# The opening of a fused attention and MLP kernel: modulation products before the transposes, loads in pieces over both queues, dummies behind gates

## The chip, the cores and the metric

The kernel runs on one core of a Trainium2 chip (trn2). The metric is the device time of one execution in microseconds (us).

Three instruction streams matter in what follows. PE is the matrix engine (TensorE), DVE the vector engine, POOL the GpSimd engine; ACT (the scalar engine) and SP (the sync engine) also issue transfers, each on a queue of its own.

## The reference, cut to what matters

```python
mod = (_silu(c) @ w_mod).reshape(c.shape[0], 6, 1, -1)
sa, ca, ga, sb, cb, gb = ...                     # six vectors of 512
h = _layernorm(x, axis=-1) * (1 + ca) + sa       # x: 2048 x 512
x = x + ga * attention(h, k_cache, v_cache, wq, wo)   # 32 heads, the last 512 keys
h = _layernorm(x, axis=-1) * (1 + cb) + sb
x = x + gb * (relu(h @ w1) @ w2)
```

Before any head can be projected (q = h @ wq), the first 512 rows of x must be normalised, transposed, and scaled by `1 + ca` and shifted by `sa`. These two vectors come from `silu(c)` and the first 1,024 columns of `w_mod` (1 MB).

## The kernel before

Each engine has an instruction stream, and a small builder (`KB`) works out the semaphore waits. It walks through the program in the order of the Python calls, and keeps for each resource its last write and the reads since. An operation waits for what has been recorded up to then.

```python
for r in reads:
    req(r.w)               # the last write recorded so far; None: no wait
for w in writes:
    req(w.w)
    for ev in w.r:         # the reads recorded so far
        req(ev)
```

The opening (cut; "..." marks cuts):

```python
for i in range(2):                                   # x, tiles 0..3, in two transfers
    dma(x_sb[:, 2*i:2*i+2, :], xv[:, 2*i:2*i+2, :], f"xa{i}", writes=..., eng=ACT if i else SP)
dma(c_row[:, :], ...)                                # c, 1 KB, on SP
load_wm01(0); load_wm01(1, ACT)                      # w_mod, two halves of 512 KB
load_wq(0, 2, ACT); load_wq(2, 2); load_k(0); load_v(0)
kb.op(POOL, ... memset(ones, 1.0))
...
warm(7)                  # 7 dummy products of 512 columns on PE
silu_exp(5)              # transpose of c on PE, exp on ACT; waits for c
warm(9)                  # 9 more dummies
...
silu_mul()               # POOL: three operations, result sc_bf
ln_stat(0); ln_stat(1)   # DVE: mean and variance of tiles 0 and 1, result mv
rstd_add(0, 2); rstd_pow(0, 2)                       # DVE, then a power on POOL
ln_stat(2) ...
ln_norm(0); ln_norm(1)                               # DVE: xn
...
ln_tposes(0, TB[0])      # PE: 4 transposes of tile 0
fs = mod_cols_mm(0, QBK) # PE: 32 one-column products, w_mod x silu(c)
for f in fs: f()
ln_norm(2)
mod_cols_evac(0, QBK)    # DVE: modc, the scale and shift
for tl in range(1, TPB): ln_tposes(tl, ...)
# then: hT = xnT * scale + shift in two halves, and the projections of heads 0 and 1
```

The dummies are there for PE's clock, which starts low: at first they stand 0.43 us apart, later 0.22.

## Time and profile before

| | before |
|---|---|
| median of the first 3 runs | 560.43 us (560.34 to 561.92) |
| median of 6 runs, taken beside the changed kernel | 560.94 us (560.34 to 562.04) |
| span of the profiled run | 559.4 us |
| PE busy | 98% of the span |
| first score product (attention proper begins) | 13.34 us |

How to read it: PE is busy nearly all the time. The lines themselves stand in the prediction below. In them `psW<-ones` is a dummy, `psQ<-sc_bf,wmw` a modulation product (`wmw` is w_mod), `<-ident,xn` a transpose, `<-hT,wq` a projection and `psS<-qT,kT` a score product; psW, psQ, psO and psS are the banks that PE writes, and modc is the scale and shift. Nearly all products pass through one helper (L1372) and nearly all transposes through another (L1375). A mean clock of 1.000 is the full one.

### The profile page before, as it was taken

To read this page: it belongs to the slowest core of one execution; us is meant where nothing else is said; L and a number is where in the kernel's file an instruction comes from. 1 tells how busy PE (TensorE), PEld (TensorE's weight loads), DVE (VectorE), ACT (ScalarE), POOL (GpSimd) and SP (SyncE) were. 2 spreads that over 40 slices of the span, in tenths; PEclk is the share of its full clock that TensorE was granted. 3 is DMA by queue.
4 is the path that set the end of the run, shared out by engine and by line. 5 is a ranking of instruction groups with operands and counts; after the bars stand their busy time and mean duration, and the time that the engine had idled before them with its cause. 6 is when DMAs were issued, how large, how long until landed. Compare 5 with 4: busy or idle time off the path is not lost.

```text
span 559.4 us, 9666 instructions
## 1 busy us (share of the span) xinstructions
PE 550.5 (98%) x4060; PEld 315.8 (56%) x4134; DVE 253.8 (45%) x551; ACT 348.9 (62%) x453; POOL 54.7 (10%) x53
## 2 busy tenths in 40 slices
PE   8999999999999999999999999999999999999998
PEld 4665555555555555555555555555555654444444
DVE  4455555553546544335445443333354448321134
ACT  4986666666666666666666666666666644432500
POOL 3000022004410000033000000332000000000000
DMA  9897763513114144352352412111215110210001
GB/s 268 248 207 174 143 169 46 114 39 76 40 38 76 39 73 117 58 133 57 94 95 57 76 40 39 39 39 38 39 39 76 39 30 0 44 34 23 22 29 47
DMA packets 113309, 42.67 MB, mean 76 GB/s; under 512 B 93928, under 2 KB 112104, under 8 KB 113256
## 3 DMA queue, kind: packets, MB, share of 16 engines
q1 hardware_dynamic: 112024, 40.82, 34.3%
q10 hardware_dynamic: 1232, 1.15, 0.6%
q8 instruction: 33, 0.54, 0.4%
q14 instruction: 20, 0.16, 0.1%
HBM read 18.35 MB, written 2.10 MB: 37 GB/s over the span
## 4 chain that ended last, share of the span: by engine, by line
PE 98%; issue 1%; DMA 1%; DVE 0%; SPq 0%; DVEq 0%
PE psS L1372 28%; PE psO L1372 27%; PE psQ L1372 23%; PE psW L1372 20%; DMA c_row<-in_c_dram 1%; DVE qT L1611 0%; DVE hT L1630 0%; SPq L1303 0%; DVE PT L1723 0%; DVE PT L1725 0%; PE psS L1375 0%; PE psO L1416 0%; DVE modc L1438 0%; DVEq L123 0%
## 5 line engine op out<-in xcount | busy, mean ns | idle before, releaser
L1493 ACT ACTIVATE PT<-psS 128x1024 bf16<-128x1024 f32 x256 | 262.7, 1028 | 128.2 <-PE psS L1372 128.1
L1372 PE MATMUL psS<-qT,kT 128*128 128x512 bf16 x508 | 150.9, 379 | 0.5 <-DVE qT L1611 0.4
L1372 PEld LDWEIGHTS psO<-v,PT 128*128 128x128 bf16 x2048 | 126.6, 98 | 30.2
L1372 PE MATMUL psO<-v,PT 128*128 128x129 bf16 x2048 | 137.0, 220 | 0.0
L1372 PE MATMUL psQ<-hT,wq 128*128 128x512 bf16 (+1 forms) x510 | 130.5, 377 | 0.3 <-DVE hT L1630 0.2
L1503 DVE RECIPROCAL rinv<-psO 128x4 f32<-128x4 f32 x128 | 23.3, 182 | 227.2 <-PE psO L1372 227.2
L1372 PE MATMUL psW<-wo,oT 128*128 128x512 bf16 x454 | 118.1, 379 | 3.0
L1504 DVE TENSOR_TENSOR o<-psO,rinv 128x512 bf16<-128x512 f32 x128 | 88.5, 691 | 4.9 <-DVE rinv L1503 0.5
L1372 PEld LDWEIGHTS psQ<-hT,wq 128*128 128x128 bf16 x512 | 49.9, 98 | 60.3 <-issue 0.6
L1372 PEld LDWEIGHTS psS<-qT,kT 128*128 128x128 bf16 x512 | 49.5, 98 | 58.9 <-ACT PT L1493 0.7
L1485 ACT ACTIVATE qT<-psQ 128x512 bf16<-128x512 f32 x126 | 74.7, 593 | 0.0
L1712 ACT ACTIVATE wq<-psS 128x512 bf16<-128x512 f32 x56 | 33.4, 597 | 49.3 <-PE psS L1372 48.9
L1372 PEld LDWEIGHTS psW<-wo,oT 128*128 128x128 bf16 x512 | 45.0, 98 | 32.9 <-DVE acc L1526 1.2
L1526 DVE TENSOR_TENSOR acc<-psW,acc 128x512 f32<-128x512 f32 x48 | 33.2, 691 | 6.5 <-PE psW L1372 6.5
L1372 PE MATMUL psO<-wmw,wq 128*128 128x512 bf16 (+1 forms) x165 | 32.8, 352 | 0.3
L1529 POOL TENSOR_TENSOR acc<-acc,gaf 128x512 f32<-128x512 f32 x12 | 15.6, 1303 | 146.7 <-DVE acc L1526 139.8
L1388 POOL TENSOR_TENSOR rstd<-rstd,cst 128x4 f32<-128x4 f32 x7 | 7.2, 1025 | 216.8 <-DVE rstd L1387 216.8
L1723 DVE TENSOR_TENSOR PT<-psO,gbf 128x512 f32<-128x512 f32 (+1 forms) x12 | 7.5, 624 | 40.4 <-PE psO L1372 40.4
L1372 PE MATMUL psS<-h2T,wmw 128*128 128x512 bf16 x109 | 25.0, 379 | 0.2
L1372 PEld LDWEIGHTS psO<-wmw,wq 128*128 128x128 bf16 x168 | 15.3, 98 | 16.5
L1372 PE MATMUL psS<-hT,wmw 128*128 128x512 bf16 x110 | 24.4, 379 | 0.1
L1382 DVE BATCH_NORM_STATS2 st<-x 128x6 f32<-128x512 bf16 x31 | 21.1, 681 | 4.8 <-DMA x<-in_A_x_dram 4.8
(85 smaller groups left out, 192.6 us busy)
## 6 DMA issues: line engine op xcount, KB each, us to landing
wo<-in_A_wo_dram SPq DMA_DIRECT2D x4, 1024.0 KB, 5.9
wq<-in_A_wq_dram SPq DMA_DIRECT2D x7, 512.0 KB, 4.6
wmw<-in_B_w_dram SPq DMA_DIRECT2D x14, 256.0 KB, 3.1
wmw<-in_w_mod_dram SPq DMA_DIRECT2D x5, 512.0 KB, 4.8
oT<-o SPq DMA_TRANSPOSE x128, 2.4
out_dram<-PT SPq DMA_DIRECT2D x15, 128.0 KB, 1.7
x<-in_A_x_dram SPq DMA_DIRECT2D x3, 512.0 KB, 4.3
v<-in_A_v_cache_dram SPq DMA_DIRECT2D x8, 128.0 KB, 3.8
```

Of the source, the lines that this page charges most:

```text
L1372: kb.op(PE, lambda e: e.matmul(out_ap, lhsT, rhs, start=start, stop=stop), reads=reads, group_writes=[R_b[k] for k in bk], signal=signal)
L1382: kb.op(DVE, lambda e: e.bn_stats(st[:, t, :], x_sb[:, t, :]), reads=[R_x[t]], writes=[R_st[t]])
L1388: kb.op(POOL, lambda e: e.tensor_tensor(rstd[:, sl], rstd[:, sl], cst[:, 0:1].to_broadcast([P, hi - lo]), op=ALU.pow), reads=R_rstd[sl] + ...
L1485: kb.op(ACT, lambda e: e.activation(qT[u % NQT][:, :], bank[bk], ACTF.Copy), reads=[R_b[bk]], writes=[R_qT[u % NQT]])
L1493: kb.op(ACT, lambda e: e.activation(PT[u % NPT][:, pr * 2:pr * 2 + 2, :], s_ps[pr][:, :, :], ACTF.Exp, scale=scale), reads=[R_b[pr * 2], R ...
L1503: kb.op(DVE, lambda e: e.reciprocal(rinv[:, u, :], o_ps[:, :, P]), reads=[R_b[5], R_b[6]], writes=[R_rinv])
L1504: kb.op(DVE, lambda e: e.tensor_tensor(o_sb[u % NOS][:, :, :], o_ps[:, :, 0:P], rinv[:, u, :].unsqueeze(2).to_broadcast([P, TPB, P]), op=A ...
L1526: kb.op(DVE, lambda e: e.tensor_tensor(acc[:, tl, :], bank[WBK], acc[:, tl, :], op=ALU.add), reads=[R_b[WBK], R_acc[tl]], writes=[R_acc[tl]])
L1529: kb.op(eng, lambda e: e.tensor_tensor(acc[:, tl, :], acc[:, tl, :], gaf[:, :], op=ALU.mult), reads=[R_acc[tl], R_ga], writes=[R_acc[tl]])
L1712: kb.op(ACT, lambda e: e.activation(h1T[b % 2][:, fc, :], bank[bk], ACTF.Relu), reads=[R_b[bk]], writes=[R_h1[b % 2][fc]], pre=all_events( ...
L1723: kb.op(DVE, lambda e: e.tensor_tensor(yt[i][:, c0:c1], bank[bk][:, c0:c1], gbf[:, c0:c1], op=ALU.mult), reads=[R_b[bk], R_gb], writes=[R_ ...
```

## The change

Its intent: let the modulation products run while PE would otherwise wait for the first normalised tile; bring x and w_mod in smaller pieces so that work can begin on the first ones; keep PE occupied with dummies only as long as needed (gated by the statistics of tiles 0 and 1). The diff, cut to its core:

```diff
     def load_wm01(i, eng=None):
-        c0, c1 = i * DC // 2, (i + 1) * DC // 2
-        dma(wm01[:, c0:c1, :], wm01v[:, c0:c1, :], f"wm{i}", writes=[R_wm[i]], eng=eng)
+        dma(wm01[:, i, :], wm01v[:, i, :], f"wmc{i}", writes=[R_wmc[i]], eng=eng)
...
-    def warm(n):
+    def warm(n, gate=()):
         for i in range(n):
-            mm(bank[WBK], ones..., [R_ones], [WBK], i == n - 1)
+            mm(bank[WBK], ones..., [R_ones] + list(gate), [WBK], i == n - 1)
...
     for i in range(2):
-        dma(x_sb[:, 2 * i:2 * i + 2, :], ..., f"xa{i}", ..., eng=ACT if i else SP)
+        for t in (2 * i, 2 * i + 1):
+            dma(x_sb[:, t, :], xv[:, t, :], f"xa{t}", writes=[R_x[t]], eng=ACT if i else SP)
     dma(c_row[:, :], ...)
-    load_wm01(0)
-    load_wm01(1, ACT)
-    load_wq(0, 2, ACT)
+    for i in range(DC):
+        load_wm01(i, (ACT, SP)[i % 2])
+    for i, eng in enumerate((ACT, SP)):
+        dma(wq_sb[:, 2 * i:2 * i + 2, 0:QA * Dh], ..., f"wqa{i}", writes=[R_wqa[i]], eng=eng)
...
-    kb.op(POOL, lambda e: e.memset(ones[:, :], 1.0), writes=[R_ones])
+    kb.op(DVE, lambda e: e.memset(ones[:, :], 1.0), writes=[R_ones])
...
-    warm(7)
+    warm(10)
     silu_exp(5)
-    warm(9)
+    warm(3, [R_mv[0]])
+    warm(2, [R_mv[1]])
...
-    ln_tposes(0, TB[0])
     fs = mod_cols_mm(0, QBK)
     for f in fs:
         f()
+    ln_tposes(0, TB[0])
+    mod_cols_evac(0, QBK)
     ln_norm(2)
-    mod_cols_evac(0, QBK)
```

## The prediction

> **What bounds the kernel now.** I read the page first, for what limits the whole span, then the chain of waits for the first 14 us, the timeline of the same stretch, and last the landing times of the opening loads. The page's part 1 and part 4:
>
> ```profile
> PE 550.5 (98%) x4060; PEld 315.8 (56%) x4134; DVE 253.8 (45%) x551; ACT 348.9 (62%) x453; POOL 54.7 (10%) x53
> ...
> PE 98%; issue 1%; DMA 1%; DVE 0%; SPq 0%; DVEq 0%
> ```
>
> PE is busy 98% of 559.4 us and the chain lies on it. In the steady part one step of attention costs PE about 2.63 us (projections in the chain start at 20.82, 23.45, 26.14, 28.72), with no gap over 0.05 us. The diff touches no instruction of that part except the resources its waits name, so what it can win is the time before PE starts streaming. The chain of waits there (start us, us, what):
>
> ```profile
> 1.24 3.66 DMA c_row<-in_c_dram
> 4.90 0.05 issue
> 4.95 0.18 PE psO L1416
> 5.13 3.86 PE psW L1372 x9
> 8.98 0.22 PE psS L1375 x4
> 9.21 0.79 PE psQ L1372 x32
> 10.00 0.02 issue
> 10.02 0.18 DVE modc L1438
> ...
> 10.30 0.42 DVE hT L1630
> ...
> 12.55 0.44 DVE qT L1611
> 12.99 0.35 issue
> 13.34 0.38 PE psS L1372
> ```
>
> So the opening is 13.3 us, 2.4% of the time, and it would have to shrink by 11.2 us for a 2% gain. What stands on it: the nine dummy products (psW), which begin when c has landed and keep PE until 8.8; four transposes; the 32 modulation products; their evacuation (modc); the scaling of hT; the first projections. Is PE needed there, or only occupied? The timeline, in which the bracket tells what ended a wait:
>
> ```profile
> 6.92 0.20 POOL L1423 TENSOR_TENSOR sc_bf<-c_f,tmp 128x4 bf16<-128x4 f32 x1
> 7.08 1.51 POOL L1591 TENSOR_TENSOR rstd<-rstd,cst 128x2 f32<-128x2 f32 x2
> 7.82 1.22 DVE L1393 TENSOR_SCALAR xn<-x,mv,rstd 128x512 bf16<-128x512 bf16 x3
> 8.02 0.15 PEld L1372 LDWEIGHTS psW<-ones 128*128 128x128 bf16 x1 [0.28 <-issue]
> 8.70 0.90 POOL L1604 TENSOR_SCALAR xn<-x,s,rstd 128x512 bf16<-128x512 bf16 x1
> 9.04 0.94 PE L1372 MATMUL psQ<-sc_bf,wmw 128*128 128x1 bf16 x32
> 10.02 0.17 DVE L1438 TENSOR_TENSOR modc<-psQ,m 128x8 f32<-128x8 f32 x1 [0.98 <-PE psQ L1372]
> ```
>
> sc_bf is ready at 7.12 and the first xn at about 8.24, yet neither gets a PE slot before 8.82: dummies hold it. The loads the products need:
>
> ```profile
> wmw<-in_w_mod_dram SPq DMA_DIRECT2D x1, 512.0 KB, 6.3
> ```
>
> That half, issued at 1.66, lands at 1.66 + 6.3 = 7.96; the half on ACT's queue was issued at 1.23 and took 4.9, so 6.13. First x lands at 0.79 + 4.0 = 4.79 and 0.79 + 4.2 = 4.99.
>
> **What the Trainium skill says.** "TensorE: Matmul & The Clock Gate", Part 1, says that the array starts at half clock and gets the full one only after a busy window of about 3.4 us, in a window that runs freely. The trace agrees in effect: dummy weight loads stand at 5.46, 5.89, 6.32 ... 8.02, 0.43 us apart for 512 columns, while later 512-column products are 0.215 us apart; the granted clock nevertheless reads 1.00, so that column doesn't show it. The switch comes only near 8.5, since the first seven dummies stop at 4.2 and the wait for c breaks the window. "DMA: Bandwidth & Descriptors", "Issuing engines are not separate DMA queues", says that SP's and ACT's transfers share 16 engines, and a second queue saves issue time alone. It agrees: the windows view has these engines at 1.01 to 1.16 of busy share from 3 to 8 us, at 326 to 385 GB/s. Spreading loads only reorders bytes. The same page, "Queues, rings and completion order", has each engine consume a queue's descriptors in ring order; c (1 KB), issued right after x on SP, lands at 4.90, after x's 4.79, as that says.
>
> **The change part by part.**
> *Ones on DVE.* POOL's memset ran 0.78 to 0.98 and PE began at 1.04. DVE is free from the start; I take 0.1 us for it: PE begins near 0.93.
> *Ten dummies before the silu transpose, not seven.* Ten at 0.425 are 4.25 us: PE is free at 5.2. Before, c alone set that transpose, at 4.94. So +0.25 on the silu chain, a loss. It should also fill a clock window, so the switch comes near 5.2, or by 7.6 at worst.
> *x in four transfers, c behind two of them.* c's issue moves from 1.24 to about 1.65, yet it still follows the same 256 KB in its ring. x rows become 1 KB pieces, so I allow 0.1 to 0.4: c at 5.0 to 5.3. With PE free at 5.2, the silu transpose is at about 5.25: +0.3 on before. Tile 0 alone lands about 1 us earlier, near 3.8, and statistics finish earlier; but that buys nothing, as POOL's power for rstd stands behind the three silu operations in program order (5.43 to 7.12), and those start with c. POOL's chain so moves +0.3: sc_bf 7.42, first rstd 8.1, xn0 8.55, xn1 8.87, xn2 9.35, xn3 (before 8.70 to 9.60) 9.9.
> *Loads of w_mod in four chunks, alternating.* x and w_mod are 1.5 MB. From 1 to 7 us the windows view moved 27+215+361+385+378+366 = 1,732 KB, 1.5 MB by about 6.5; add the spread between engines and the 1 KB rows: the last chunk lands at 7.2 to 7.5 rather than 7.96, no longer mixed with wq.
> *Gated dummies.* Three wait for tile 0's statistics (ready), two for tile 1's (about 6.0). At the half clock they end at 7.5, at the full one at 6.5. Neither holds xn0 back.
> *Products ahead of the transposes.* They run 7.5 to 8.35, beside POOL and DVE instead of on the path; their evacuation comes after xn1 in DVE's order, 8.77 to 8.95.
> Then: transposes of tile 1 done about 9.35, so the first half of hT starts near 9.4, against 10.28: -0.9. The transposes of tile 3 wait for POOL's xn3 at 9.9 and are done at 10.35, so the second half starts at 10.4 (before 10.95). Three DVE scalings 0.32 apart end at 11.45; the last four second-half products of 0.109 end their stream at 12.0, the qT cast runs 12.2 to 12.6 (before 12.99 to 13.41): 0.8 us earlier.
>
> Sum: products and evacuation off the path -1.0, dummies that held the first transpose (8.82 against 8.24 + 0.2) -0.4, later c and silu +0.3, tile 3 through POOL as the new limit +0.3: -0.8 us. From there PE streams as before, all of it reaching the end: 560.43 - 0.8 = 559.6.
>
> **The rivals.** (1) The silu chain eats it: if c lands at 5.8, behind 256 small pieces, everything behind POOL moves by 0.9 and the gain is about 0.2: 560.2. For it: c's landing is on the chain already, and its ring isn't shortened. Against: it comes behind the same bytes. (2) The last w_mod chunk stays at 8.0: the products end at 8.85 and now stand ahead of the transposes, so tile 0 waits 0.3; but the second half hangs on xn3 at 9.9, so only 0.1 is lost: 559.7. (3) Cold clock: fewer dummies (15 for 16), maybe a pause before 7.5. If the first projections ran at 0.213 instead of 0.109 each, 16 would cost 1.7 us more: 561.3. Against: over 6 us of nearly unbroken dummies hold a full window at most phases. (4) POOL is not the limit as I have it, or the switch comes so early that all is ready sooner: the gain is 1.2 and the time 559.2. (5) Later loads hide the gain: the third projection needs wq for heads 2 and 3 (landed about 9.2) and kT (about 9.8), both ahead of 12.2; SP issues kT some 1.3 us later, behind three more issues, so it stays inside. I give that little.
>
> **Range and chances.** -0.8 with half a microsecond of doubt from c, the phase of the clock window (which can also shorten the dummies of before in some runs) and the spread of three runs (560.34 to 561.92). Nothing is 11 us large. 558.9 to 560.5 should hold it; within 2% almost surely.
>
> **What would show it.** In the changed profile: ten dummies from about 0.93; c or the tenth dummy as what released the silu transpose at about 5.25; sc_bf at 7.4; 32 products before 8.5, beside POOL; the first scaling of hT near 9.4; the last transposes waiting on POOL's xn; the first score product near 12.5; the same 2.63 us step behind it; span about 558.6. I am wrong if c lands past 5.6, if the products wait past 8.0 for w_mod, if projections come 0.21 apart, or if the opening gets shorter and the span doesn't.

## The result, and the profile after

The changed kernel takes 563.11 us at the median (562.78 to 563.69, 6 runs) against 560.94 us of the kernel before (6 runs); the ratio is 1.0037, with a 95% interval of 1.0023 to 1.005. It is about 2.1 us slower where 0.8 us faster was forecast. The change stays inside 2%, but the sign is wrong and the time lies above the range.

The profiled run spans 561.0 us. The chain of waits of the changed kernel (start us, us, what), to be held against the chain of before in the prediction:

```profile
2.20 7.41 DMA wmw<-in_w_mod_dram
9.61 0.05 issue
9.65 0.57 PE psQ L1373 x16
10.22 0.02 issue
10.24 0.17 DVE modc L1439
10.41 0.33 DVE xn L1394
...
11.64 0.85 PE psQ L1373 x4
12.49 1.71 PE psO L1373 x8
14.20 0.61 PE psQ L1373 x4
14.81 0.21 issue
15.02 0.38 PE psS L1373
```

Two things are to be seen. The chain now hangs on a transfer of w_mod, which is issued at 2.20 and lands at 9.61; before, the later half of w_mod was issued at 1.66 and was there at 7.96. (In front of the lines shown, from 0.80 to 2.20, ACT issues two pieces of x and the first chunk, one after another: more pieces also mean a later issue.) And the eight half-width projections into psO take 1.71 us; in the chain of the run that changed only the order, which is shown further down, the same eight take 0.89. The first score product comes at 15.02 instead of 13.34: 1.68 us later, and the span is 561.0 - 559.4 = 1.6 us longer. So all of it is in the opening. From the first score product to the end both kernels take 546 us (559.4 - 13.34 = 546.1; 561.0 - 15.02 = 546.0).

Why do the projections take twice as long? The windows view of the changed kernel gives, for each stretch, the length, then the busy time (and number of instructions) of PE, weight loads, DVE, ACT and POOL, then the granted clock of PE, the busy share of the DMA engines, and GB/s:

```profile
6.00:7.00 1.00, 0.25 (x2) 0.00 (x0) 0.93 (x4) 0.97 (x3) 0.92 (x2) 1.00 0.84 311
7.00:8.00 1.00, 0.00 (x0) 0.00 (x0) 0.93 (x4) 0.31 (x2) 0.76 (x2) 1.00 1.08 352
...
11.00:12.00 1.00, 1.00 (x11) 0.88 (x9) 0.76 (x3) 1.00 (x3) 0.00 (x0) 0.51 1.23 243
12.00:13.00 1.00, 1.00 (x7) 0.69 (x6) 0.73 (x3) 0.63 (x2) 0.00 (x0) 0.50 1.09 335
13.00:14.00 1.00, 1.00 (x7) 0.69 (x6) 0.00 (x0) 0.38 (x1) 0.00 (x0) 0.50 1.22 294
```

PE does nothing from 6.25 to beyond 8, and from about 11.0 its clock is granted at 0.50, until about 14.4. The records of the clock in this trace put the half-clock stretch at 11.03 to 14.44: 3.41 us. In that stretch start all but the last of the 16 half-width projections of the first two heads (11.43 to 14.54).

The timelines of PE part the 1.68 us. The first projection starts at 11.43 instead of 10.86, 0.57 us later; from there to the first score product it is 3.59 us instead of 2.48, 1.11 us more. So in this one run the late start costs about a third and the half clock about two thirds.

The third view is the timeline of the changed kernel:

```profile
1.11 3.84 PE L1373 MATMUL psW<-ones 128*128 128x512 bf16 x10 [1.11 <-DVE ones L1571]
...
4.88 0.17 PE L1417 MATMUL psO<-ident,c_row 4*128 4x4 bf16 x1
...
4.99 1.26 PE L1373 MATMUL psW<-ones 128*128 128x512 bf16 x5
...
5.92 0.18 DVE L1384 BATCH_NORM_AGGREGATE mv<-st 128x2 f32<-128x6 f32 x1 [1.71 <-PE psW L1373]
...
6.85 0.20 POOL L1424 TENSOR_TENSOR sc_bf<-c_f,tmp 128x4 bf16<-128x4 f32 x1
...
8.41 0.75 PE L1373 MATMUL psQ<-sc_bf,wmw 128*128 128x1 bf16 x16 [2.16 <-DMA wmw<-in_w_mod_dram]
...
9.65 0.55 PE L1373 MATMUL psQ<-sc_bf,wmw 128*128 128x1 bf16 x16 [0.49 <-DMA wmw<-in_w_mod_dram]
```

The five "gated" dummies run straight behind the silu transpose and take 1.26 us together: they wait for nothing. The line at 5.92 shows the opposite of a gate: the statistics of tile 0 (whose first step ended at 4.21) stood still for 1.71 us until dummies (psW) had run. That is the builder's rule from above. `warm(3, [R_mv[0]])` is called before `ln_stat(0)`, so no write of mv is recorded yet and the read waits for nothing; the later write of mv then has to wait for the reads. The gate points backwards.

So there were three suspects: the late w_mod, the fall of the clock, and the backward gates.

### The profile page after: what moved, and what is told of

Same layout as the page of the kernel before. It is cut to its first block, busy times and chain, and to the rows that moved or that the text cites. A ratio compares the mean times of both kernels' runs of the same rounds, so it can differ in the third digit from the quotient of the medians. Undisturbed runs are those within 1.5% of the kernel's fastest.

```text
span 561.0 us, 9673 instructions
## 1 busy us (share of the span) xinstructions
PE 550.4 (98%) x4059; PEld 316.5 (56%) x4133; DVE 253.9 (45%) x552; ACT 349.1 (62%) x453; POOL 54.5 (10%) x52
## 4 chain that ended last, share of the span: by engine, by line
PE 97%; DMA 1%; issue 1%; ACTq 0%; DVE 0%
PE psS L1373 28%; PE psO L1373 27%; PE psQ L1373 23%; PE psW L1373 19%; DMA wmw<-in_w_mod_dram 1%; ACTq L1303 0%; PE psS L1376 0%; DVE xn L1394 0%; DVE PT L1727 0%; DVE PT L1729 0%; PE psW L1376 0%; DVE modc L1439 0%
```

## The experiments

Each changes the kernel before or the changed kernel by a few lines; all results were correct. The theory (T in the expectations) was that the loss comes from the late w_mod and from the clock together. The rivals: late loads alone (L), the clock alone (C), the backward gates (G), the order (O).

### First round

**e_fill.** The changed kernel, more dummies.

```diff
     warm(2, [R_mv[1]])
+    warm(14)
```

> The changed kernel with 14 more dummy products behind the gated ones, nothing else. Theory T (the 2 us come from two things: the clock of TensorE falls to half from 11.0 to 14.4 us because PE stands idle from 6.2 to 8.4, and the last chunk of w_mod lands at 9.6): granted clock 1.00 throughout, projections 0.109 us apart again, span about 559.4, ratio to before 0.999 to 1.001; the modulation products still wait for w_mod until about 9.6. Rival L (late loads alone cost it, the clock is incidental): nothing gained, ratio stays near 1.0037. Rival C (the clock alone costs it): ratio 0.999 or lower, with products not late.

Measured: 562.57 us, ratio 1.003 (1.0017 to 1.0043), clock 1.00 in all five runs. In the profiled run, the fastest of the five (span 559.8), the clock went as T has it: the projections were 0.109 us apart and the first score product came at 13.51. But w_mod landed at about 9.1, and what the products waited for were the dummies, which ended at 9.18. The mean is far worse than that run. Fourteen dummies take 14 x 0.22 = 3.1 us at full clock and 14 x 0.43 = 6.0 us at half, and in the traces the clock rises anywhere from 3.8 to 13.3 us; a fixed number of dummies may so pay back what it buys. That this is what made the other four runs slow is not shown, since only one was traced. By its ratio, T missed.

**e_oldloads.** The changed kernel with the opening loads of before.

```diff
-    x in four transfers, w_mod in four, wq for heads 0 and 1 in two
+    x in two transfers, w_mod in two halves, wq for heads 0 and 1 in one (as before)
```

> The changed kernel with the opening loads of before (x in two transfers, w_mod in two halves, wq for two heads in one), dummies and order as changed. Theory T: w_mod lands near 8.0, the products run 8.0 to 8.8, the projections start about 1.3 us earlier than in the changed kernel; PE still idles from 6.2 to 8.0, so the clock may still fall, at a moment when fewer projections are left: ratio 1.000 to 1.002. Rival L: back to before or better, 0.998 to 1.000, even if the clock falls. Rival C: clock below 1.00 and ratio still 1.003.

Measured: 562.07 us, ratio 1.0017 (1.0005 to 1.0029). w_mod landed at 8.00 and the products ran from 8.14 to 9.1, about as expected. Of six runs five had a mean clock of 0.997 and took 561.91 to 562.95 us; the sixth had 1.000 and took 560.98. One kernel, one chip, and the runs whose clock fell lie 562.31 - 560.98 = 1.3 us above the one whose clock did not. (This is not the fall alone: the moment at which the clock first rises also differs from run to run and sets how long the dummies last.) The profiled run also showed the backward gates at work: its clock rose only at 6.9, so the dummies were slow, and the statistics behind them waited until 7.17. From there the chain runs through the statistics to the transposes, not through w_mod.

**e_fill_oldloads.** Both undone.

```diff
     (loads as in e_oldloads)
     warm(2, [R_mv[1]])
+    warm(9)
```

> The changed kernel with the loads of before and 9 more dummies (to about 8.0 us): both suspected causes undone, the products still ahead of the transposes. Theory T: the gain that was predicted appears, clock 1.00, span about 558.6, ratio 0.998 to 0.999. If a third cause exists, the ratio stays at 1.000 or above.

Measured: 561.28 us, ratio 1.0009 (0.9996 to 1.0022), clock 1.00 in all runs. T missed here too. The profiled run had a span of 558.8, close to the 558.6 that the prediction promised, but it was the fastest of five; the spans went up to 560.1. In it the gain that was predicted is there; what takes it away in the other runs was not traced. Even in this run the chain passes through a backward gate: the aggregate of tile 0 starts at 5.85, released by dummies that end at 5.75.

**e_newloads_only.** The kernel before with only the changed loads.

```diff
-    x in two transfers, w_mod in two halves, wq for heads 0 and 1 in one
+    x in four transfers, w_mod in four, wq for heads 0 and 1 in two (as changed)
```

> The kernel before with only the changed opening loads (x in four transfers, w_mod in four chunks, wq for two heads in two, over both queues). Its dummies run until about 8.8 and the transposes stand ahead of the products. Theory T: products finish at about 10.05 instead of 9.85 since the last chunk lands near 9.6, clock stays 1.00, ratio 1.0003 to 1.001. Rival L: the whole loss, 1.003 to 1.004. Rival C: 1.000 or below.

Measured: 561.15 us, ratio 1.0004 (0.9991 to 1.0016). The last chunk landed at about 9.8 and the products ended near 10.3, about as expected. Late w_mod by itself is nearly free under the old order. In the profiled run it does set the pace (the first score product comes at 13.61, 0.27 us later than in the trace of before), but four transposes go ahead of it and the clock stays up, although the dummies ended at 7.1. Rival L, as a cause by itself, falls.

### Second round

**e_order_only.** The kernel before with only the changed order.

```diff
-    ln_tposes(0, TB[0])
     fs = mod_cols_mm(0, QBK)
     for f in fs:
         f()
+    ln_tposes(0, TB[0])
+    mod_cols_evac(0, QBK)
     ln_norm(2)
-    mod_cols_evac(0, QBK)
```

> The kernel before with one edit: the 32 modulation products and their evacuation ahead of the transposes of tile 0. Theory T (the order is harmless, the loss comes from the loads and the clock): products start when the dummies end (about 8.8 at the half clock) and end by 9.6, the first half of hT is scaled some 0.1 to 0.2 us earlier, ratio 0.9993 to 1.000. Rival O (the order itself costs it, since the transposes now wait behind w_mod): ratio 1.001 or more.

Measured: 560.54 us, ratio 0.9994 (0.998 to 1.0007), clock 1.00. The order is harmless and perhaps worth 0.3 us, which is within the noise. Lines of its chain of waits:

```profile
1.65 6.18 DMA wmw<-in_w_mod_dram
...
7.97 0.95 PE psQ L1372 x32
...
10.77 0.89 PE psO L1372 x8
...
12.26 0.59 PE psS L1372 x2
```

The products now wait for w_mod (7.83) and nothing else, and the scores begin at 12.26. That run's clock had risen by about 3.9 us, so that its nine dummies were over at about 7. In the trace of before that the prediction was read from, the clock rose only near 8.8 and the dummies held PE until then. The spread of the kernel before may well come from this; only one run of it was traced, so that is not shown.

**e_realgate.** The changed kernel with the gates recorded after what they name.

```diff
-    warm(3, [R_mv[0]])
-    warm(2, [R_mv[1]])
...
     ln_stat(0)
     ln_stat(1)
+    warm(3, [R_mv[0]])
+    warm(2, [R_mv[1]])
```

> The changed kernel with the two gated groups of dummies recorded after the statistics they name, so that the wait goes the meant way. As changed, the builder sees these reads of mv before anything writes it: the dummies wait for nothing, and the writing of mv waits for the dummies (in the changed profile the aggregate of tile 0 starts at 5.92, 1.7 us after its statistics, released by PE psW). Theory T: that inversion was hidden behind w_mod at 9.6 and the clock, so the aggregate moves to about 4.4, xn0 to about 7.8, and the time stays: ratio 1.002 to 1.004. Rival G (the inverted wait is the cause): ratio 1.000 to 1.001.

Measured: 562.88 us, ratio 1.0038 (1.0024 to 1.0052). The aggregate of tile 0 moved from 5.92 to 4.61, right behind its statistics, and nothing was won: the first xn began at 8.36 (8.02 in the changed kernel), and the last chunk landed at about 9.7. In the profiled run the clock fell for two windows (9.13 to 15.96). The backward gates are a real error in the code, but rival G falls as the cause of this loss. Where w_mod is on time they do show: the chains of e_oldloads, e_fill_oldloads, e_after_xpairs and e_dummies_only pass through them; what they cost there was not measured by itself.

**e_wmchunks.** The kernel before with w_mod in four chunks, nothing else.

```diff
-    load_wm01(0)
-    load_wm01(1, ACT)
+    for i in range(DC):
+        load_wm01(i, (ACT, SP)[i % 2])
```

> The kernel before with w_mod in four chunks over both queues and nothing else of the loads changed; one look at when the last chunk lands. If the chunks themselves are what comes late: 9.0 or later. If it is the four transfers of x ahead of them: 8.2 or earlier. The time of one run decides nothing.

Measured: one run of 560.79 us (state unknown). The last chunk on SP's queue, from the issues view (tile, queue, size, us from issue to landing), issued at 2.05:

```profile
wmw<-in_w_mod_dram SPq DMA_DIRECT2D x1, 256.0 KB, 5.4
```

It lands at 2.05 + 5.4 = 7.4. In this run, then, the chunks are not what comes late. That left the four transfers of x, or the split of wq.

**e_best1.** A first try at a better version: changed order, loads of before, real gates, and dummies that wait for sc_bf.

```diff
     (loads as in e_oldloads, gates as in e_realgate)
+    warm(3, [R_sc])
```

> The changed kernel with the loads of before, the gates made real, and three more dummies that wait for sc_bf (near 7.1). Theory T: no statistic waits for a dummy, no window of the clock stays empty, w_mod lands by 8.0: clock 1.00, span 558.3 to 558.9, ratio 0.997 to 0.999 on the mean and with less spread than the version with 9 unconditional dummies, since these ended later whenever the clock rose later. If the ratio stays at 1.000 or above, something else in the order costs what it wins.

Measured: 560.83 us, ratio 1.0003 (0.9989 to 1.0016); clock 1.00 in all five runs. The profiled span of 558.7 fell in the expected range; the ratio did not, so T missed.

### Third round

**e_keepclock.** The changed kernel, gates made real, ten dummies in the idle stretch.

```diff
     (gates as in e_realgate)
+    warm(5, [R_sc])
+    warm(5, [R_wmc[0]])
```

> The changed kernel with real gates (as in the run that mended them alone, ratio 1.0038) and ten more dummies whose waits let them fill the idle stretch and nothing else: five wait for sc_bf, five for the first chunk of w_mod (8.2 to 8.4). They end before the last chunk lands at 9.6. This leaves the late loads and takes away the clock's fall. Theory T: clock 1.00 in all runs, projections 0.109 apart, ratio 1.0005 to 1.0015, so the clock is worth some 1.5 us of the 2. Rival L: no change, 1.003 to 1.004.

Measured: 562.0 us, ratio 1.0019 (1.0006 to 1.0032), clock 1.00 in all five runs. Against e_realgate (1.0038) the held clock is worth half of the loss, some 1.1 us of 2.1. That is less than the 1.5 us expected. The windows view shows the projections at full clock:

```profile
11.00:12.00 1.00, 1.00 (x12) 0.74 (x13) 1.00 (x4) 1.00 (x3) 0.00 (x0) 1.00 1.24 244
12.00:13.00 1.00, 1.00 (x10) 0.90 (x11) 0.66 (x3) 0.95 (x3) 0.00 (x0) 1.00 1.08 337
```

From 12 to 13 us PE has ten products, where the changed kernel had seven. Its first projection starts at 11.43, exactly when it does in the changed kernel, and its first score product comes at 13.93 instead of 15.02: in these two traces the half clock is worth 1.09 us. What is left, 1.0019, is put down to the late w_mod under the new order; a little of it (the ten dummies ended at 9.4, so the first 16 products, whose chunks had landed by 8.5, started later than they could, and all 32 ended at 10.37 instead of 10.20) is the experiment's own.

**e_dummies_only.** The kernel before with only the changed dummies.

```diff
-    kb.op(POOL, ... memset(ones, 1.0))
+    kb.op(DVE, ... memset(ones, 1.0))
-    warm(7)
+    warm(10)
     silu_exp(5)
-    warm(9)
+    warm(3, [R_mv[0]])
+    warm(2, [R_mv[1]])
```

> The kernel before with only the changed dummies (ones filled by DVE, ten ahead of the silu transpose, three and two behind it, gates inverted as in the change); its loads and order as before. Theory T: PE idles from about 6.2 to 8.2 here too, so a window without dense products follows and the clock falls in a part of the runs (mean clock 0.997), ratio 1.001 to 1.003. Rival L: 1.000 or less, because w_mod lands by 8.0.

Measured: 563.14 us, ratio 1.004 (1.0027 to 1.0053): this one part makes the whole loss, with w_mod on time, and more than the 1.001 to 1.003 that T gave. The clock fell in all five runs: its mean was 0.997 in two runs (562.11 and 562.63 us) and 0.994 in three (563.14 to 563.64 us). From its windows view:

```profile
6.00:8.00 2.00, 0.11 (x1) 0.00 (x0) 1.86 (x7) 1.15 (x4) 1.54 (x3) 1.00 1.11 344
...
12.00:13.00 1.00, 1.00 (x6) 0.70 (x5) 0.00 (x0) 0.38 (x1) 0.00 (x0) 0.50 1.16 311
```

PE has 0.11 us of work in the two microseconds from 6 to 8; in the trace of before the same view has 2.00. Then the clock falls (10.75 to 14.16 in the records). The first projection starts earlier than in the trace of before (10.39 against 10.86), and yet the first score product comes later (14.07 against 13.34).

**e_after_xpairs.** The changed kernel with only x in two transfers again.

```diff
-        for t in (2 * i, 2 * i + 1):
-            dma(x_sb[:, t, :], xv[:, t, :], f"xa{t}", ...)
+        dma(x_sb[:, 2 * i:2 * i + 2, :], xv[:, 2 * i:2 * i + 2, :], f"xa{i}", ...)
```

> The changed kernel with x in two transfers of two tiles again; w_mod in four chunks and wq in two stay. The look at the chunks alone had the last one at 7.43, the kernels with four transfers of x have it at 9.2 to 9.8. Theory T with the loads' part narrowed to x: last chunk by 7.7, products by 8.5; the clock may still fall, since PE idles from about 6.2 and the gates are still inverted: ratio 1.000 to 1.002. If the last chunk lands at 9 or later, x is not what delays it and the split of wq is left.

Measured: 561.96 us, ratio 1.0018 (1.0004 to 1.0033). The last chunk landed at about 8.5: over 1 us earlier than with four transfers of x, but not the 7.7 expected, nor the 7.4 of e_wmchunks. Again one kernel shows both clocks: 561.09 and 560.46 us at 1.000, 561.92 to 563.23 us at 0.997. The means differ by 562.38 - 560.78 = 1.6 us.

**e_best2.** e_best1 with w_mod in four chunks.

```diff
     (x, wq as before; w_mod in four chunks; gates as in e_realgate)
+    warm(3, [R_sc])
```

> A version meant to beat both: products ahead, w_mod in four chunks over both queues, x in two transfers, wq as before, real gates, three dummies that wait for sc_bf. Theory T: last chunk near 7.4, products 7.6 to 8.5, second projections 0.3 us earlier than in the version with the loads of before, clock 1.00, span 558.2 to 558.7, ratio 0.9980 to 0.9995.

Measured: 561.05 us, ratio 1.0 (0.9987 to 1.0013), span 559.5; T missed. The chunks landed at up to about 8.8 here, with the same opening loads as e_wmchunks. What one look at the chunks had shown is not dependable.

### Fourth round

**e_fewer.** The kernel before with six dummies less.

```diff
-    warm(9)
+    warm(3)
```

> The kernel before with six dummies less behind the silu transpose (7 and 3 in place of 7 and 9), nothing else. It parts the number of dummies from the other things that the change does to them (ones on DVE, ten ahead, inverted gates). Theory T (the idle stretch between the last dummy and the dense projections lets the clock fall, or not rise): projections at 0.213 us in the profile, ratio 1.002 to 1.005. Rival I (the inverted gates or the ten ahead cost it): ratio 0.999 to 1.001.

Measured: 562.44 us, ratio 1.003 (1.0017 to 1.0043). In the profile, the first projections are 0.213 us apart: the clock rose only near 13.3. So fewer dummies alone, without any gates and with the ones filled by POOL, can cost as much as the whole change. But they do it by another way, a late rise; e_dummies_only loses by a fall after an early rise, and this run doesn't part the gates and the ones from that. (The granted-clock column reads 1.00 throughout in this run: it does not show the half clock from which an execution starts, only later falls. The records of the clock begin at the first rise, and this trace, that of before, e_newloads_only and e_wmchunks have none.)

**e_keepclock_oldorder.** e_keepclock with the old order.

```diff
     (e_keepclock)
+    ln_tposes(0, TB[0])          # ahead of the products, as before
```

> The changed kernel with real gates and the ten late dummies that held its clock (ratio 1.0019), and with the order of before: transposes of tile 0 ahead of the products. The changed loads alone cost 1.0004 under the old order. Theory T with the order as a part: when w_mod is late, the new order puts the transposes and the third tile's normalisation behind it, so the old order gives back 0.5 us or more: ratio 1.0003 to 1.0012. If it stays at 1.0019, the order is free and the late dummies or the loads cost it.

Measured: 562.43 us, ratio 1.0032 (1.0019 to 1.0045): worse, where better was expected. Its chain shows why this is no clean test: the late dummies ended at about 9.9 only, past the last chunk (9.4), and both the transposes and the products stood behind them. The run says that my late dummies cost something, not what the order costs.

**e_xtiles.** The kernel before with x in four transfers, nothing else.

```diff
-        dma(x_sb[:, 2 * i:2 * i + 2, :], xv[:, 2 * i:2 * i + 2, :], f"xa{i}", ...)
+        for t in (2 * i, 2 * i + 1):
+            dma(x_sb[:, t, :], xv[:, t, :], f"xa{t}", ...)
```

> The kernel before with x in four transfers and nothing else; one look at when the two halves of w_mod land. If the four transfers of x delay w_mod: the later half lands at 8.8 or later in place of 7.8 to 8.0. If not, by 8.2, and then only the combination with the four chunks brings 9.2 to 9.8. The time of one run decides nothing.

Measured: one run of 564.66 us (state unknown, mean clock 0.994). The half of w_mod on SP's queue, issued at 2.12, in the issues view:

```profile
wmw<-in_w_mod_dram SPq DMA_DIRECT2D x1, 512.0 KB, 8.1
```

The two halves landed at about 10.2 and 10.0, instead of 7.96 at the latest. In this run, then, splitting x was enough to delay w_mod by 2 us, while the first pieces of x came earlier (by 3.5 instead of 4.79).

**e_best3.** Dummies sized to end by 8.2 whenever the clock rises.

```diff
     (order as changed, loads as before)
-    warm(10)
+    warm(8)
     silu_exp(5)
+    warm(3)
...
     ln_stat(1)
+    warm(3, [R_mv[1]])
+    warm(3, [R_sc])
```

> A second try at a version that beats both: loads of before, products ahead, and dummies sized so that they end by 8.2 whenever the clock rises: eight, then three behind the silu transpose, three that wait for tile 1's statistics, three that wait for sc_bf. Theory T: clock 1.00 in all runs, spans 558.4 to 559.2, ratio 0.9985 to 0.9997. At 1.000 or above, the order has nothing more to win on the mean than the 0.9994 of the order alone.

Measured: 560.53 us, ratio 1.0 (0.9987 to 1.0014), clock 1.00 in all six runs. No gain.

### Last round: the table of the three parts

**e_after_olddummies** and **e_after_oldorder.** The changed kernel with one part undone each.

```diff
-    warm(10) ... warm(3, [R_mv[0]]); warm(2, [R_mv[1]]); ones by DVE
+    warm(7)  ... warm(9); ones by POOL                     # e_after_olddummies
```

```diff
+    ln_tposes(0, TB[0])          # ahead of the products     e_after_oldorder
     fs = mod_cols_mm(0, QBK)
```

> The changed kernel with the dummies of before (ones by POOL, seven ahead of the silu transpose, nine ungated behind it); changed loads and changed order stay. Theory T (the dummies carry the loss): clock 1.00, last chunk of w_mod still at 9.2 to 9.8, projections 0.109 apart, ratio 1.0000 to 1.0012. Rival P (late loads under the new order cost more than half, as the 1.0019 of the version with late dummies suggests): ratio 1.0015 to 1.003.

> The changed kernel with the order of before (transposes of tile 0 and the third normalisation ahead of the products); changed loads and dummies stay. Theory T: the order is neither cause nor cure; the clock falls, ratio 1.0030 to 1.0048. If the order is what costs: 1.002 or less.

Measured: e_after_olddummies 562.86 us, ratio 1.0037 (1.0024 to 1.0049), clock 0.997 in all five runs: T missed, and its rival had the larger part right but not far enough. e_after_oldorder 562.89 us, ratio 1.0033 (1.0018 to 1.0049), as T expected; its one run at clock 1.000 took 560.97 us, three at 0.997 took 562.67 to 562.97, two at 0.994 took 563.29 and 563.43.

Two lines of the windows view of e_after_olddummies show what happened in its profiled run:

```profile
8.00:10.00 2.00, 0.85 (x28) 0.80 (x29) 0.10 (x1) 0.00 (x0) 0.91 (x2) 1.00 2.10 238
...
12.00:13.00 1.00, 1.00 (x7) 0.68 (x5) 0.53 (x2) 0.60 (x2) 0.00 (x0) 0.50 1.08 331
```

With the dummies of before, PE idles as well: for 0.57 us per microsecond from 8 to 10. All nine dummies ran at full clock here and ended by 6.8; with the products first in line and w_mod landing at 9.6, nothing dense followed until 11.3, and the clock fell.

The eight combinations of loads (L), order (O) and dummies (D), each as in the changed kernel where it is named:

| parts changed | ratio to before | mean clock of the runs |
|---|---|---|
| none | 1 | mostly 1.000 |
| O | 0.9994 | 1.000 |
| L | 1.0004 | 1.000, one 0.999 |
| D | 1.0040 | 0.997 and 0.994 |
| O and D | 1.0017 | 0.997, one 1.000 |
| L and O | 1.0037 | 0.997 |
| L and D | 1.0033 | 0.997 and 0.994, one 1.000 |
| all (the change) | 1.0037 | 0.997, one 0.994 |

The ratios of rows from different rounds each refer to the kernel before in their own round, and each round ran on another chip. The rows do not add up, and they need not: every slow row has the fallen clock. The table suggests two ways into it, fewer dummies (D) and w_mod late with everything queued behind it (L and O); one is enough, and having both costs no more than one. It has five or six runs a row, and the moment at which the clock rises was not controlled, so some of the difference between rows may be luck. Why O and D together cost less than D alone is open.

What decides the fall can be read closer from the records. In all seven traces with a fall it comes one or two times 3.41 us after the rise, so the clock is judged in stretches of that length counted from the rise. An estimate of the work in each stretch, from the spacings in these traces (0.218 us for a dummy at the full clock, 0.109 for a projection, 0.055 for a transpose; the one-column products left out): where PE had 1.2 us of work or less in a stretch, the half clock followed (seven of seven), and after every stretch with 1.4 us or more the full clock stayed, in all traces that have records. The changed kernel had 13 transposes, 0.7 us, in its stretch from 7.61 to 11.03. In e_after_xpairs PE ran no dummy and no projection for 4.0 us (6.33 to 10.36), longer than the whole stretch, but eight projections still fell before the end of theirs at 11.20, and the clock stayed. So it is not one pause that costs the clock but a stretch with too little in it, and where the stretches lie differs from run to run.

## Why the prediction was wrong, point by point

**The step that failed first: the loads.** "The last chunk lands at 7.2 to 7.5 rather than 7.96." It landed at 9.6 to 9.8 in the changed kernel. The prediction divided the bytes by the rate of before, and the rate did not hold: from 4 to 5 us the changed kernel moved 170 GB/s at a DMA share of 0.57, where the kernel before had 385 at 1.06. (The prediction read that share as 1.01 to 1.16 from 3 to 8 us; its view has 1.00 to 1.16.) But the rate is not all: e_newloads_only, with the same loads, moved 308 GB/s from 2 to 8 us against 339 of before and 269 of the changed kernel, and its last chunk landed just as late, at 9.85. Rival 2 had the chunk at 8.0 at worst. The runs point to x: with x in two transfers the four chunks landed at 7.4 to 8.8 (three kernels), with four transfers at 9.1 to 9.8 (the changed kernel and the seven others that have its loads), and the two halves at 10.0 to 10.2. Why four smaller transfers of x leave the engines without work afterwards is open; no run here tells it.

**The step that cost most: PE's clock.** Rival 3 named the effect and nearly its size (1.7 us), and then was argued away: "over 6 us of nearly unbroken dummies hold a full window at most phases". That looks at the rise alone. The clock did rise, at 4.2 us, earlier than in the trace of before; then the dummies ran at twice the speed and were over at 6.25, and the clock *fell* again at 11.0 for 3.41 us after PE had done next to nothing dense. The faster the dummies run, the sooner they stop protecting the clock. Its worth: the traces of the changed kernel and of e_keepclock differ by 1.09 us behind the same first projection, and the ratios of e_realgate and e_keepclock by 1.1 us. Read inside single kernels whose runs differ in the clock, it is 1.3 us (e_oldloads), 1.6 us (e_after_xpairs) and 562.82 - 560.97 = 1.9 us (e_after_oldorder, for 0.997); two of these three rest on a single run at the full clock, and the time of the rise differs too. So the clock is half of the 2.1 us or more. With the clock held throughout (e_keepclock), 1.0019 remains, some 1.1 us, which is put down to the late w_mod.

**The gates.** "Three wait for tile 0's statistics (ready), two for tile 1's (about 6.0)." They wait for nothing; the statistics wait for them. The diff was read for what it says, not for what the builder makes of it in call order. It cost nothing measurable here (e_realgate, 1.0038 against 1.0037); w_mod came later than all of it.

**The order.** "Products and evacuation off the path -1.0" and "dummies that held the first transpose -0.4". Alone, the order gave 0.9994, some 0.3 us (560.9 x 0.0006). The direction was right, the size was not. One reason stands in the traces: the prediction was read from one in which the clock rose late, near 8.8, and the dummies lasted until then; in the profile of e_order_only it rose at 3.9. The prediction laid the late rise on the wait for c, which follows the first seven dummies. But e_order_only begins with the same seven dummies and the same wait, so it is the run that differs, not the program. The other is that the prediction compared with that one trace (span 559.4), while the spans of before went down to 558.4.

**What was pessimistic, and what held.** c, which was put at 5.0 to 5.3, was not waited for at all: the silu transpose came at 4.88 (5.25 said), straight behind the tenth dummy, and the last dummies already ran at full clock; sc_bf was ready at 7.05 (7.42 said). None of this could help with w_mod at 9.6. The step that held is the last one: what the opening loses reaches the end undiminished, 1.68 us there and 1.6 us in the span.

No version tried here beats the kernel before clearly. The best is the order alone, 0.9994 with an interval of 0.998 to 1.0007; e_best2 and e_best3, with clock and loads in order, came to 1.0. As far as these runs tell, what remains to be won in the opening is smaller than the spread of the kernel before (spans of 558.4 to 560.5).

## What to carry to other kernels

Ask of dummies not only whether they raise the clock but what keeps it up afterwards: they shrink to half their time when they succeed, so they should be tied to the event they bridge to and not counted, and no stretch of 3.41 us, wherever it begins, should be left with too little work. In the five versions that tied them so (e_keepclock, e_keepclock_oldorder, e_best1 to e_best3) the mean clock was 0.999 or 1.000 in every run; none of them was clearly faster than the kernel before. Where dependencies are derived from call order, a wait on something not yet written is no wait but a wait the other way round; look in the timeline for who released whom. And do not price a split transfer by its bytes: look where the transfers behind it land.

## What the Trainium skill lacked or had wrong

- "TensorE: Matmul & The Clock Gate", "Why this matters for your kernels", advises no PE-idle gaps over about 3 us between bursts of matmuls. That is not enough: here the clock fell though PE's longest pause was about 2.2 us (6.25 to 8.41 in the changed kernel), and in the traced run of e_dummies_only it was also 2.2 us (6.11 to 8.35). The length of the fall agrees with the window that the page gives: 3.41 us in four of the traces, two windows (6.83 us) in e_realgate, e_after_oldorder and e_xtiles. What the page lacks is how much work a window needs: by the estimate above, the clock fell after windows with 1.2 us or less and stayed after those with 1.4 us or more. It also doesn't warn that a counted row of dummies ends sooner once the clock is up (0.22 us each in place of 0.43) and so can leave the next window nearly empty.
- The mean clock that a profile gives does not show the half clock at the start: e_fewer reads 1.00 while its first projections stand 0.213 us apart. No page was found that says it.
- "DMA: Bandwidth & Descriptors", "Rules for kernel authors", says to coalesce small transfers and that those under 64 KB pay mostly overhead. It has nothing on what small transfers do to large ones behind them: splitting x from 2 x 256 KB into 4 x 128 KB had the w_mod behind it land at 10.0 to 10.2 us instead of 7.96 (one look), and at 9.6 to 9.8 in the changed kernel.
